# Gated mix of linear attention and a squared-ReLU block on one core: the second piece of the first chunks issued from ScalarE's queue

## The chip, the core and the metric

The kernel runs on one core of a Trainium2 chip. The metric is the device time in microseconds (us) of one execution; the kernel before was run three times. One further execution was taken by the hardware profiler, and all lines of a profile shown here come from such an execution. Engines are TensorE (PE in the profile, its weight loads PEld), VectorE (DVE), ScalarE (ACT), GpSimd (POOL) and SyncE (SP); SPq and ACTq are the instructions with which SyncE and ScalarE issue transfers.

## The reference

The input x has 2048 rows (tokens) of 448 numbers, all float32. Two branches are computed from it and mixed with a gate for each token:

```python
x = A_x
g = _sigmoid((x * gate_w).sum(-1, keepdims=True))
a = _A_ref(x, A_wqkv, A_wo)                    # linear attention, 16 heads of 28
b = _B_ref(x, B_w1, B_b1, B_w2, B_b2)          # relu(x @ w1 + b1)**2 @ w2 + b2, hidden width 1792
return g * a + (1 - g) * b
```

In the attention branch q and k go through phi(t) = where(t > 0, t + 1, exp(t)) + 1e-6; then kv = sum over tokens of phi(k) v, z = sum of phi(k), and the output is phi(q) kv / (phi(q) z + 1e-6), multiplied by wo.

## The kernel before

All inputs are float32. Each operand of a matmul is split into a high part, rounded to the matmul's type float32r, and a low part, the rest; a product is then three matmuls (high by high, low by high, high by low). ScalarE mostly makes the high part (`split_hi`, line 66, or line 68 on VectorE), VectorE the low part (`split_lo`, line 71).

The 448 input features lie in four chunks of up to 128 (c = 0 to 3, the last one holds 64 features twice), the tokens in four blocks of 512 (b = 0 to 3), and the hidden width in 14 tiles of 128. The program opens with the up projection (x by w1) of block 0: six hidden tiles (`NS = 6`), each with a PSUM bank of its own, `first[0]` to `first[5]`, called h_ps in the profile. Chunk 0 goes first, with 128-row matmuls at lines 685 and 216, then chunk 1; chunks 2 and 3 follow from a queue of parts that `work_off` emits at line 300, in two halves of 64 rows. After that come keys, down projection, attention and the other blocks; the stores end the program.

The order in which each engine runs its instructions is the order in which the code is written (`manual_schedule`). At the head of the program it is this:

- TensorE runs 14 matmuls on constants (line 177, `warm_ps`), which need no data.
- SyncE issues the loads through `load` (line 59). The first two (lines 181 to 183) are the pieces of xw. Piece n is a tile `xwr` of 128 partitions by 512 numbers: 256 columns of x, chunk 0 (the tokens of one half of block 0), beside 256 columns of w1, chunk 0 (two of the hidden tiles 0 to 3). Then follow w1 for the hidden tiles 4 to 6, chunk 0 (`w1r` from w1b), and for chunks 1 to 3 a piece of x (`xr`) and two of w1 (`w1r` from w1a and w1b).
- Lines 680 to 688 take piece 0 and then piece 1: VectorE casts the x columns to `xh` (line 681), ScalarE makes the high part of the two weight tiles (line 683), TensorE multiplies hidden tiles 0 and 1 by these columns (line 685), VectorE subtracts to get `xl` (line 686), and TensorE multiplies with that (line 688, by way of line 216). Line 690 then makes the low part of the weights from both pieces, line 691 splits the third load, and lines 692 to 696 run the rest of chunk 0 on six hidden tiles.

Each engine works in order. A transfer tells its end by one of eight semaphores in turn, so that SyncE's eighth and later transfers each wait until the one that had the semaphore before has landed.

Of the kernel before, what the change touches and what calls it, by code (L numbers as in the profile page):

```python
# [33 lines left out]
def gated_mix_kernel(ctx: ExitStack, tc: tile.TileContext, xw, xt, xn, wk, wq, wv, wo, w1a, w1b, w2, b1, b2, gw,  # L34
                     kvmask, out):
    nc = tc.nc
    act, dve, pool, pe, sp = nc.scalar, nc.vector, nc.gpsimd, nc.tensor, nc.sync
# [15 lines left out]
    def slot(shape, dt, name):  # L53
        return work.tile(shape, dt, name=name, tag="s", bufs=NSLOT)
# [3 lines left out]
    def load(dst, src):  # L58
        loader[0].dma_start(out=dst, in_=src)
# [70 lines left out]
    def load_w1(h, g, c):  # L130
        w1_raw[h, g, c] = slot([P, (TB, 3 * P)[g]], F, f"w1r{h}{g}{c}")
        load(w1_raw[h, g, c], (w1a, w1b)[g][h, c])
# [47 lines left out]
    xw_raw = []  # L180
    for n in range(2):
        xw_raw.append(slot([P, TB], F, f"xwr{n}"))
        load(xw_raw[n], xw[n])
    load_w1(0, 1, 0)
    for c in range(1, 4):
        load_x(0, c)
# [763 lines left out]
```

## Time and profile before

| | us |
|---|---|
| median of 3 runs | 420.62 (420.17 to 420.63) |
| profiled execution, its own time | 420.09 |
| its span, first to last instruction | 418.3 |
| TensorE busy in the span | 414.2 |
| VectorE, ScalarE, GpSimd busy | 274.6, 173.2, 87.5 |
| first use of xw piece 0, piece 1 (from the span's start) | 3.43, 4.42 |

The granted clock of TensorE is given as 1.000 over the span. In a row of the timeline stand the start, the duration, the engine, the line, the operation with the tile written and the tiles read, the count of instructions merged, and in brackets the idle time of the engine before it and what ended it. In the list of waits stand the engine and line that waited, for whom, and three numbers: us in total, times, the longest in us. A busy TensorE is not TensorE at its peak, since matmuls overlap; the distance from start to start tells the pace.

### The profile page before, as it was taken

What the parts mean: (1) busy time and instruction counts of PE and PEld (TensorE: products, weight loads), DVE (VectorE), ACT (ScalarE), POOL (GpSimd) and SP (SyncE); (2) the same over time, 40 slices, a digit from 0 to 9 for tenths busy, and PEclk for the clock granted to TensorE, in tenths of its full rate; (3) what the DMA queues carried; (4) which work ended last, traced back from release to release, by engine and by line L of the source; (5) the groups of instructions that cost most, each with busy time, mean ns of one, the idle gap of its engine ahead of it and who ended that gap; (6) DMA issues with size and microseconds to landing.
All of it is one profiled execution on the core that took longest, in us unless ns stands there. A gap on an engine that the chain in (4) does not pass through costs nothing.

```text
span 418.3 us, 9312 instructions
## 1 busy us (share of the span) xinstructions
PE 414.2 (99%) x3836; PEld 402.4 (96%) x3836; DVE 274.6 (66%) x520; ACT 173.2 (41%) x305; POOL 87.5 (21%) x166
## 2 busy tenths in 40 slices
PE   9999999999999999999999999999999999999996
PEld 6899999999999999999999999999999999999996
DVE  5887737682476827576379886678843975558734
ACT  6965335451044621445234653325530363314720
POOL 0015300140003400035830498200402013110000
PEclk9999999999999999999999999999999999999999
DMA  8805500050001610006541155210402013010002
GB/s 272 259 8 146 182 2 5 6 194 2 2 5 32 198 46 2 3 19 203 171 133 43 31 89 154 66 44 2 127 2 88 2 23 107 19 70 2 2 2 88
DMA packets 12634, 29.81 MB, mean 71 GB/s; under 512 B 3136, under 2 KB 6176, under 8 KB 12592
## 3 DMA queue, kind: packets, MB, share of 16 engines
q0 software_dynamic: 8416, 22.76, 18.2%
q1 hardware_dynamic: 4032, 6.37, 4.7%
q8 instruction: 30, 0.49, 0.5%
q14 instruction: 12, 0.10, 0.1%
q10 hardware_dynamic: 144, 0.10, 0.1%
HBM read 23.28 MB, written 4.20 MB: 66 GB/s over the span
## 4 chain that ended last, share of the span: by engine, by line
PE 99%; DVE 0%; issue 0%
PE o_ps L300 30%; PE h_ps L300 30%; PE k_ps L300 9%; PE g_ps L300 8%; PE a_ps L300 8%; PE q_ps L300 7%; PE h_ps L216 2%; PE o_ps L881 1%; PE kv_ps L300 1%; PE warm_ps L177 1%; PE m_ps L300 1%; PE last_ps L82 0%; PE h_ps L685 0%; DVE last L898 0%
## 5 line engine op out<-in xcount | busy, mean ns | idle before, releaser
L300 PE MATMUL h_ps<-xh,w 64*128 64x512 f32 x709 | 160.0, 387 | 0.0
L300 PE MATMUL o_ps<-w,hh 64*128 64x448 f32 x848 | 153.0, 359 | 0.0
L300 PEld LDWEIGHTS o_ps<-w,hh 64*128 64x128 f32 x848 | 124.9, 184 | 2.6
L300 PE MATMUL h_ps<-xl,w 64*128 64x512 f32 x395 | 124.8, 387 | 0.0
L300 PE MATMUL o_ps<-w,hl 64*128 64x448 f32 x424 | 124.3, 360 | 0.0
L300 PEld LDWEIGHTS h_ps<-xh,w 64*128 64x128 f32 x709 | 107.5, 184 | 0.9 <-ACT w L66 0.4
L300 PEld LDWEIGHTS o_ps<-w,hl 64*128 64x128 f32 x424 | 74.7, 184 | 1.4
L300 PEld LDWEIGHTS h_ps<-xl,w 64*128 64x128 f32 x395 | 65.0, 184 | 0.2
L221 ACT ACTIVATE hr<-h_ps,b_s 128x512 f32<-128x512 f32 x56 | 38.1, 680 | 61.0 <-PE h_ps L300 61.0
L300 PE MATMUL k_ps<-wk_s,xh 64*128 64x512 f32 x216 | 59.1, 386 | 0.0
L68 DVE CAST hh<-hr 128x512 fp32r<-128x512 f32 x56 | 23.5, 420 | 33.7 <-ACT hr L222 32.7
L300 PE MATMUL k_ps<-wk_s,xl 64*128 64x512 f32 x120 | 40.3, 386 | 0.0
L71 DVE TENSOR_TENSOR hl<-hr,hh 128x512 fp32r<-128x512 f32 x56 | 39.0, 697 | 1.9
L300 PE MATMUL q_ps<-xh,wq_s 64*128 64x512 f32 x160 | 39.7, 387 | 0.0
L425 POOL DMA_DIRECT2D qd<-q x16 | 8.8, 550 | 147.1 <-DVE q L421 147.1
L300 PE MATMUL a_ps<-m_s,qh 64*128 64x448 f32 x216 | 38.6, 359 | 0.0
L222 ACT ACTIVATE hr<-hr 128x512 f32<-128x512 f32 x56 | 35.4, 633 | 1.8
L300 PE MATMUL g_ps<-pl,nh 64*128 64x448 f32 x128 | 36.1, 359 | 0.0
L300 PE MATMUL g_ps<-ph,nh 64*128 64x448 f32 x128 | 36.1, 358 | 0.0
L300 PEld LDWEIGHTS k_ps<-wk_s,xh 64*128 64x128 f32 x216 | 35.2, 184 | 0.4
L300 PEld LDWEIGHTS a_ps<-m_s,qh 64*128 64x128 f32 x216 | 33.0, 184 | 1.4
L300 PE MATMUL a_ps<-m_s,ql 64*128 64x448 f32 x120 | 32.3, 359 | 0.0
(132 smaller groups left out, 685.0 us busy)
## 6 DMA issues: line engine op xcount, KB each, us to landing
xr<-in_xt POOLq DMA_DIRECT2D x24, 256.0 KB, 3.0
xnr<-in_xn POOLq DMA_DIRECT2D x16, 224.0 KB, 3.8
out<-out POOLq DMA_DIRECT2D x12, 224.0 KB, 2.2
w2r<-in_w POOLq DMA_DIRECT2D x9, 224.0 KB, 3.0
m_s<-m POOLq DMA_DIRECT2D x24, 56.0 KB, 2.5
w2r<-in_w SPq DMA_DIRECT2D x5, 224.0 KB, 6.8
wkr<-in_wk SPq DMA_DIRECT2D x4, 256.0 KB, 4.3
w1r<-in_w1a POOLq DMA_DIRECT2D x4, 256.0 KB, 3.5
```

The lines of the kernel that those rows point to most:

```text
L68: eng.tensor_copy(hi, src)
L71: eng.tensor_tensor(lo, src, f32(hi), op=ALU.subtract)
L177: pe.matmul(warm_ps[:, :256], warm[:, :P], warm, start=True, stop=True)
L216: ins = pe.matmul(ps, a, m, start=(c == 0 and n == 0), stop=False)
L221: act.activation(r, ps, AF.Relu, bias=b1_s[:, f:f + 1])
L222: act.activation(r, r, AF.Square)
L300: ins = pe.matmul(out, a, m, start=start, stop=stop)
L425: pool.dma_start(out=q_t[b][i], in_=q)
L881: ins = pe.matmul(total.ps[:, :D], a[:, i * P:(i + 1) * P], w[:, k], start=False, stop=f == NF - (3 if i == 3 else 1) and n == 2)
```

## The change

The second piece of xw is issued by ScalarE, as the first instruction of its program, and no longer by SyncE. The first piece stays on SyncE, now by a direct call in place of `load`. Sizes, tiles and all that is computed are the same.

```diff
     xw_raw = []
     for n in range(2):
         xw_raw.append(slot([P, TB], F, f"xwr{n}"))
-        load(xw_raw[n], xw[n])
+        (sp, act)[n].dma_start(out=xw_raw[n], in_=xw[n])
     load_w1(0, 1, 0)
```

SyncE's program at its head, as a difference (xwr_102 is piece 0, xwr_104 piece 1, w1r_106 the up weights of the hidden tiles 4 to 6 for chunk 0, xr_1_108 chunk 1 of x):

```order
 L946 UNCONDITIONAL_BRANCH
-L59 DMA xwr_102<-in_xw 128x512
-L59 DMA xwr_104<-in_xw 128x512
+L183 DMA xwr_102<-in_xw 128x512
 L59 DMA w1r_106<-in_w1b 128x384
 L59 DMA xr_1_108<-in_xt 128x512
```

One issue leaves, and every load behind it stands one place earlier.

ScalarE's program at its head before, with the semaphores that an instruction waits for (DMAHW0 is piece 0's landing, DMAHW1 piece 1's; w_00 is the split weight tile of the hidden tiles 0 to 3, w_01 that of 4 to 6):

```order
L946 UNCONDITIONAL_BRANCH [waits barrier_Pool_Activation_PE_DVE_SP_release]
L66 ACT_TABLE_LOAD
L66 ACTIVATE w_00_166<-xwr_102 128x128 [waits DMAHW0_49]
L66 ACTIVATE w_00_166<-xwr_102 128x128
L66 ACTIVATE w_00_166<-xwr_104 128x128 [waits DMAHW1_49]
L66 ACTIVATE w_00_166<-xwr_104 128x128
L66 ACTIVATE w_01_185<-w1r_106 128x384 [waits DMAHW2_49]
```

and with the change:

```order
L946 UNCONDITIONAL_BRANCH [waits barrier_Pool_Activation_PE_DVE_SP_release]
L183 DMA xwr_104<-in_xw 128x512
L66 ACT_TABLE_LOAD
L66 ACTIVATE w_00_166<-xwr_102 128x128 [waits DMAHW0_49]
L66 ACTIVATE w_00_166<-xwr_102 128x128
L66 ACTIVATE w_00_166<-xwr_104 128x128 [waits DMAHW1_49]
L66 ACTIVATE w_00_166<-xwr_104 128x128
L66 ACTIVATE w_01_185<-w1r_106 128x384 [waits DMAHW2_49]
```

The issue of piece 1 stands ahead of the table load; ScalarE's other instructions keep their order, and so do all of TensorE's, VectorE's and GpSimd's.

## Prediction

> **What bounds the kernel now.** I read the page first: its totals and its chain of waits.
>
> ```profile
> span 418.3 us, 9312 instructions
> PE 414.2 (99%) x3836; PEld 402.4 (96%) x3836; DVE 274.6 (66%) x520; ACT 173.2 (41%) x305; POOL 87.5 (21%) x166
> PE 99%; DVE 0%; issue 0%
> ```
>
> TensorE is busy from its first to its last instruction, and the chain that ended last runs through it alone. So this change can move the end only by moving TensorE's stream. The list of waits, taken for TensorE's weight loads over the whole program, says how often anything holds that stream up:
>
> ```profile
> PEld L177 <- issue: 0.8, 1, 0.8
> PEld h_ps L685 <- ACT w L66: 0.4, 1, 0.4
> PEld h_ps L300 <- ACT w L66: 0.4, 1, 0.4
> PEld o_ps L881 <- issue: 0.3, 1, 0.3
> PEld h_ps L685 <- DVE xh L68: 0.2, 1, 0.2
> PEld h_ps L216 <- DVE xl L71: 0.2, 1, 0.2
> ```
>
> There are six waits in 418 us. Three of them (L685 twice, L216 once) belong to the first chunk, which is what the two pieces of xw feed. Next I read the timeline of the first 14 us (start, duration, engine, line, operation):
>
> ```profile
> 0.75 1.28 ACT L66 ACT_TABLE_LOAD   x1 [0.75 <-PEq L942]
> 0.75 0.86 SPq L59 DMA_DIRECT2D xwr<-in_xw  x2
> 0.78 3.00 PE L177 MATMUL warm_ps<-const-bfloat16-1.0 128*128 128x256 bf16 x14 [0.78 <-PEq L942]
> 1.65 0.42 SPq L59 DMA_DIRECT2D w1r<-in_w1b  x1
> ...
> 3.43 0.51 ACT L66 ACTIVATE w<-xwr 128x128 fp32r<-128x128 f32 x2 [1.40 <-DMA xwr<-in_xw]
> 3.43 0.29 DVE L68 CAST xh<-xwr 128x256 fp32r<-128x256 f32 x1 [3.43 <-DMA xwr<-in_xw]
> 3.76 0.42 DVE L71 TENSOR_TENSOR xl<-xwr,xh 128x256 fp32r<-128x256 f32 x1
> 3.84 0.34 PEld L685 LDWEIGHTS h_ps<-xh,w 128*128 128x128 f32 x2 [0.40 <-ACT w L66]
> ...
> 4.42 0.51 ACT L66 ACTIVATE w<-xwr 128x128 fp32r<-128x128 f32 x2 [0.48 <-DMA xwr<-in_xw]
> 4.42 0.29 DVE L68 CAST xh<-xwr 128x256 fp32r<-128x256 f32 x1 [0.24 <-DMA xwr<-in_xw]
> ...
> 4.75 0.42 DVE L71 TENSOR_TENSOR xl<-xwr,xh 128x256 fp32r<-128x256 f32 x1
> 5.09 0.75 DVE L71 TENSOR_TENSOR w<-xwr,w 128x256 fp32r<-128x256 f32 x2
> 5.23 0.51 PE L216 MATMUL h_ps<-xl,w 128*128 128x256 f32 x2
> 5.37 0.53 ACT L66 ACTIVATE w<-w1r 128x384 fp32r<-128x384 f32 x1 [0.44 <-DMA w1r<-in_w1b]
> 5.57 0.63 PE L216 MATMUL h_ps<-xh,w 128*128 128x512 f32 x2
> 5.93 0.56 DVE L71 TENSOR_TENSOR w<-w1r,w 128x384 fp32r<-128x384 f32 x1
> 6.50 1.30 PE L216 MATMUL h_ps<-xh,w 128*128 128x512 f32 x5
> 6.52 0.63 ACT L66 ACTIVATE xh<-xr 128x512 fp32r<-128x512 f32 x1 [0.62 <-DMA xr<-in_xt]
> 7.18 0.69 DVE L71 TENSOR_TENSOR xl<-xr,xh 128x512 fp32r<-128x512 f32 x1 [0.69 <-ACT xh L66]
> 12.63 0.39 PE L216 MATMUL h_ps<-xh,w 128*128 128x512 f32 x1
> 12.94 0.50 PE L300 MATMUL h_ps<-xh,w 64*128 64x512 f32 x2
> ```
>
> The reader should see the relay. Piece 0 lands and is used at 3.43, piece 1 at 4.42. After each landing VectorE casts x and subtracts: piece 1's low part ends at 4.75 + 0.42 = 5.17, and TensorE takes it at 5.23. From 5.57 matmuls start one behind the other, 0.23 us apart: the five at 6.50 span 1.30, the last lasts 0.39 like the single one at 12.63, so (1.30 - 0.39) / 4. At the step from 12.63 to 12.94 only 0.31 - 0.23 = 0.08 us is spare, and the list of waits has nothing behind it but 0.3 us near the end. So **whatever the first chunk loses or wins at 5.23 arrives at the end almost whole**; there is no idle time later in TensorE's stream that could swallow more than about 0.1 us.
>
> **Are the transfers limited by issuing or by moving bytes?** The summary of the tile xwr and the table of windows answer it (in the table: the window, each engine's busy time, the granted clock, the DMA engines' busy share, GB/s):
>
> ```profile
> L59 SPq DMA_DIRECT2D xwr<-in_xw x2: 381/401/421, 0.7 to 1.2; - x2
> DMA to landing us min/median/max: 2.7/2.9/3.2
> 2.00:3.00 1.00, 1.00 (x7) 0.72 (x5) 0.00 (x0) 0.03 (x1) 0.00 (x0) 1.00 0.97 270
> 3.00:4.00 1.00, 0.92 (x6) 0.47 (x5) 0.53 (x2) 0.51 (x2) 0.00 (x0) 1.00 0.99 324
> 4.00:5.00 1.00, 0.97 (x6) 0.70 (x6) 0.73 (x3) 0.51 (x2) 0.00 (x0) 1.00 1.06 293
> 8.00:9.00 1.00, 1.00 (x7) 0.81 (x5) 0.97 (x2) 0.89 (x2) 0.00 (x0) 1.00 1.05 393
> ```
>
> The second issue starts about 0.45 us behind the first, yet its data lands 0.99 us behind (4.42 - 3.43). Between 2 and 5 us the DMA engines are 97 to 106% busy. So piece 1 waits behind piece 0's bytes, not for SyncE: 0.5 MB take what they take. In-order service is worth something here, because the early piece is whole at 3.43 while the other still moves.
>
> **The change part by part.** *SyncE:* one issue less at its head, so the nine loads behind it issue about 0.45 us earlier. That is worth nothing by itself: the queue already runs ahead of busy DMA engines, and the chunk 1 data they bring has cover (VectorE's first use is 7.18 + 0.69 = 7.87, while TensorE comes to it at about 8.55: 6.50 plus nine matmuls of 0.23).
>
> *ScalarE:* one issue more, ahead of its table load. The nearest row is ScalarE's own issue at the end of the program, beside SyncE's:
>
> ```profile
> L899 SPq DMA_DIRECT2D out<-last x1: 357/357/357, 415.0 to 415.0; - x1
> L899 ACTq DMA_DIRECT2D out<-last x1: 372/372/372, 415.5 to 415.5; - x1
> ```
>
> So 0.37 to 0.42 us. The table load moves from 0.75 to about 1.2 and ends at about 2.5, under the 1.40 us that ScalarE sits idle before 3.43. Cost nothing; without that cover it would be 0.4 us.
>
> *The landings:* this carries the sum. Both pieces are now issued at 0.75, from two queues, to DMA engines that are full. If the engines take turns between the queues, each piece gets half the rate and both are complete about when the second is now. Piece 1 wins nearly nothing; **piece 0 loses up to 0.99 us**. Everything on ScalarE and VectorE waits in order for piece 0 first. VectorE's work from piece 0's landing to piece 1's low part is then unbroken: 0.75 (3.43 to 4.18), 0.04 between instructions, 0.75 (4.42 to 5.17), together 1.54 us. With T0 for piece 0's landing the low part ends at T0 + 1.54, and TensorE shifts by T0 + 1.54 - 5.17 = **T0 - 3.63**, as long as piece 1 lands within 0.79 us of piece 0.
>
> T0 from both sides: at the present rate both land at 4.42, a shift of +0.79. If two queues move bytes at the 393 GB/s of the 8 to 9 us row instead of the 296 that the rows from 2 to 5 us average, 524 kB take 1.33 us instead of 1.77, so T0 = 3.98 and the shift is +0.35. ScalarE's piece may also start later by d: then, roughly, T0 = 4.42 - d and T1 = 4.42 + d, and the shift is the larger of 0.79 - d and d, which is never under 0.40. I take the middle, T0 = 4.20: **+0.57 us**.
>
> What hides the rest: ScalarE's four weight casts end at 4.20 + 1.04 = 5.24, before its next data at 5.37. VectorE runs 0.57 late into 5.93, and its idle 0.69 before 7.18 takes that up; without it, chunk 1 would be late by as much, still ahead of TensorE's need. TensorE's own delay has no cover. The sum for the profiled execution is 420.09 (span 418.3 and 1.8 around it) + 0.57 = 420.66; that execution lies 0.53 under the median of the runs, 420.62, so the forecast is 420.62 + 0.57 = **421.2 us, 0.14% longer**. A measurement of this kernel tells 0.2% (0.84 us) from no change, so that counts as no change.
>
> **The rivals.**
>
> *A, both pieces come early.* If the queues do not hinder each other, both land at 3.43: the low part ends at 3.43 + 1.54 = 4.97, a gain of 0.20 us, 420.4. VectorE's chain forbids more. For it: the rate of 270 to 324 GB/s early against 393 later leaves room. Against it: the busy share of 97% and more. 10%.
>
> *B, piece by piece as now.* The engines finish the first queue's rows before they turn to the other: 3.43 and 4.42 stay, shift 0, 420.6. For it: piece 0 has only 128 rows of 2 KB, few for each DMA engine. Against: nothing in the trace shows two loading queues at once. 15%. In the Trainium skill, "DMA: Bandwidth & Descriptors", section "Queues, rings and completion order", the engine changes queue only at the end of a packet, typically 9 to 17 descriptors; by that rule a piece could pass undivided and this rival would hold. No row here shows it.
>
> *C, ScalarE's piece is overtaken.* If its queue starts late enough that the up-weight load of SyncE (w1r) also goes ahead, piece 1 takes that load's landing, 5.37 in place of 4.42: shift 0.95, 421.6, slower. It decides from 0.84 us of lateness, T1 at 5.26. For it: SyncE's loads now follow 0.45 us sooner. Against: the ACTq row is as quick as the SPq row. 13%.
>
> *D, TensorE's pace drops.* The summary of line 177 gives the warm-up's matmuls (shortest, median and longest time in ns, first and last start):
>
> ```profile
> L177 PE MATMUL warm_ps<-const-bfloat16-1.0 x14: 278/417/417, 0.8 to 3.5; 128*128 128x256 bf16 x14
> ```
>
> Fourteen starts of 256 columns between 0.78 and 3.5 are 0.21 us apart, while 512 columns later take 0.23: TensorE begins at half pace. Its idle time after the warm-up grows from under 0.1 us (3.78 to the load at 3.84) to about 0.8 (3.78 to 3.84 + 0.77). If that gap keeps or puts it back at half pace for another stretch of 2.7 us, the price is 1.35 us on top of 0.57: 422.5, slower by 0.45%. For it: the warm-up ends right where the data now arrives. Against: TensorE already tolerates its idle first 0.78 us and gaps of 0.2 to 0.4. 10%. In the Trainium skill, "TensorE: Matmul & The Clock Gate", section "Part 1: The HAM clock gate", the full clock comes after a busy window of about 3.4 us and goes after an idle one; a gap of 0.8 us is no idle window, so by that rule the rival holds only where the first full window falls across the gap. The half pace until 3.5 agrees with it.
>
> **How the numbers follow.** Forecast (shared engines, +0.35 to +0.79) 52%, A 10%, B 15%, C 13%, D 10%. The likeliest gives 421.2. The range must hold A with some scatter (the runs shown differ by 0.46 us) and C, and may leave D out: 420.3 to 422.0. Slower by over 0.2%: D 10%, most of C 11%, and the part of the forecast that scatter lifts over 0.84, 8%: 29%. Faster by over 0.2%: no mechanism reaches it, 3% for what I do not see. The rest, 68%, lies within.
>
> **What would show it.** In the changed profile's timeline: ScalarE's and VectorE's first use of xwr between 3.98 and 4.42 instead of 3.43 is the sharing step; 3.43 with 4.42 unchanged is B; 3.43 for both is A. VectorE's second cast following its first subtraction without a wait for DMA shows the 1.54 us chain; a DMA wait there up to 5.3 is C. TensorE's first 512-column matmul at 5.57 + 0.57 = about 6.1, and the step to L300 at about 13.5 instead of 12.94, show that the delay is kept. Matmuls of 512 columns further apart than 0.23 us after 6 us would be D. The forecast is wrong if piece 0 still lands at 3.43, or if the later stream starts late by another amount than the first chunk.

## The result and the profile after

Over ten runs each, the changed kernel has a median of 421.95 us (420.54 to 422.51), the kernel before 420.25 (419.94 to 420.63). The ratio is 1.0032 with a 95% interval of 1.0024 to 1.0041: slower, by more than the 0.2% that this kernel's measurement can tell from no change. The ten times of the changed kernel do not lie around their median. Three are at 420.54, 420.55 and 420.80, seven between 421.77 and 422.51, and none between.

The profiled execution of the changed kernel took 422.41 us, with a span of 420.6: one of the seven. Its list of waits for TensorE's weight loads (us in total, times, longest):

```profile
PEld h_ps L685 <- ACT w L66: 1.1, 1, 1.1
PEld L177 <- issue: 0.8, 1, 0.8
PEld h_ps L300 <- ACT wk_s L66: 0.4, 1, 0.4
PEld o_ps L881 <- issue: 0.3, 1, 0.3
```

The three small waits of the first chunk have become one of 1.1 us. From the timeline of the changed kernel's first 16 us, a selection of its rows (start, duration, engine, line, operation):

```profile
0.75 0.38 SPq L183 DMA_DIRECT2D xwr<-in_xw  x1
0.75 0.41 ACTq L183 DMA_DIRECT2D xwr<-in_xw  x1
0.78 3.15 PE L177 MATMUL warm_ps<-const-bfloat16-1.0 128*128 128x256 bf16 x14 [0.78 <-PEq L942]
1.19 1.28 ACT L66 ACT_TABLE_LOAD   x1 [1.19 <-PEq L942]
4.18 0.91 ACT L66 ACTIVATE w<-xwr 128x128 fp32r<-128x128 f32 x4 [1.71 <-DMA xwr<-in_xw]
4.18 0.29 DVE L68 CAST xh<-xwr 128x256 fp32r<-128x256 f32 x1 [4.18 <-DMA xwr<-in_xw]
4.62 0.77 PE L685 MATMUL h_ps<-xh,w 128*128 128x256 f32 x2 [0.69 <-ACT w L66]
4.86 0.28 DVE L68 CAST xh<-xwr 128x256 fp32r<-128x256 f32 x1
5.17 0.43 DVE L71 TENSOR_TENSOR xl<-xwr,xh 128x256 fp32r<-128x256 f32 x1
6.47 1.05 PE L216 MATMUL h_ps<-xh,w 128*128 128x512 f32 x2
7.32 1.05 PE L216 MATMUL h_ps<-xl,w 128*128 128x512 f32 x2
8.17 1.90 PE L216 MATMUL h_ps<-xh,w 128*128 128x512 f32 x5
10.15 0.62 PE L216 MATMUL h_ps<-xh,w 128*128 128x512 f32 x2
15.24 0.50 PE L300 MATMUL h_ps<-xh,w 64*128 64x512 f32 x2
```

Piece 0 is used at 4.18 instead of 3.43, and VectorE's second cast at 4.86 shows no wait: piece 1 was there by then. TensorE has nothing to do from 3.93 to 4.62. After that comes what the profile before did not have: pairs of 512-column matmuls start 0.85 us apart (6.47, 7.32, 8.17), 0.43 for each, nearly twice the 0.23 of before. Only from about 9.4 us (8.17 and three steps of 0.43) do they come 0.23 apart. The step to line 300 stands at 15.24 instead of 12.94, 2.30 us late, and the span is longer by the same 2.3: nothing later gave or took any. The views give the granted clock as 1.000 in this profile too, so in them the half pace is seen in the starts of the matmuls alone.

The DMA engines of the changed kernel, by stage (window, busy time of each engine, granted clock, busy share, GB/s), and then its two queues between 2.5 and 4 us (packets, MB, share of 16 engines; q1 is SyncE's queue, q10 ScalarE's):

```profile
2.00:3.00 1.00, 1.00 (x7) 0.73 (x5) 0.00 (x0) 0.47 (x1) 0.00 (x0) 1.00 0.62 176
3.00:4.00 1.00, 0.93 (x5) 0.32 (x3) 0.00 (x0) 0.00 (x0) 0.00 (x0) 1.00 1.04 397
```

```profile
q1 hardware_dynamic: 155, 0.27, 48.2%
q10 hardware_dynamic: 142, 0.26, 45.4%
```

Between 2.5 and 4 us the two queues get the DMA engines about half and half. The first microsecond of moving is slower than before (176 GB/s against 270), the second faster (397 against 324).

### The profile page after: what moved, and what is told of

It is laid out like the page before. It is cut to its first block, busy times and chain, and to the rows that moved or that the text cites. A ratio compares the mean times of both kernels' runs of the same rounds, so it can differ in the third digit from the quotient of the medians.

```text
span 420.6 us, 9312 instructions
## 1 busy us (share of the span) xinstructions
PE 415.9 (99%) x3836; PEld 404.0 (96%) x3836; DVE 274.6 (65%) x520; ACT 173.0 (41%) x305; POOL 87.0 (21%) x166
## 4 chain that ended last, share of the span: by engine, by line
PE 98%; DMA 1%; DVE 0%; ACT 0%; issue 0%
PE o_ps L300 30%; PE h_ps L300 30%; PE k_ps L300 9%; PE g_ps L300 8%; PE a_ps L300 8%; PE q_ps L300 7%; PE h_ps L216 2%; PE o_ps L881 1%; DMA xwr<-in_xw 1%; PE kv_ps L300 1%; PE m_ps L300 1%; PE last_ps L82 0%; PE h_ps L685 0%; DVE last L898 0%; ACT w L66 0%
```

## The experiments

There were two questions. Why do seven of ten executions lose 1.5 to 2.3 us when the late data alone should cost 0.55 (4.18 - 3.63)? And is piece 0 late because bytes of piece 1 move beside it?

### Filling the idle time with warm-up matmuls

```diff
-    for _ in range(14):
+    for _ in range(18):
         pe.matmul(warm_ps[:, :256], warm[:, :P], warm, start=True, stop=True)
```

> The changed kernel with 18 instead of 14 warm-up matmuls, so that TensorE has work from 0.78 to about 4.57 us and is idle only briefly before the first chunk's matmuls at about 4.62. Theory P (pace): the profile of the changed kernel starts 512-column matmuls 0.43 us apart until 9.43 us and 0.23 after, because the idle time from 3.72 to 4.62 made TensorE keep its half pace for a further stretch; the late data alone costs 0.55 us (first use of both pieces at 4.18, T0 - 3.63). With the gap filled, P expects no execution with the half pace beyond about 7 us, all runs between 420.4 and 421.3, median about 420.8. Rival L (landing): the whole 1.7 us comes from the data's lateness and what follows from it on ScalarE and VectorE; it expects no change from the changed kernel, median about 422.0 with runs up to 422.5.

Measured: median 420.62, eleven runs between 420.43 and 421.19, ratio to the kernel before 1.0011 (1.0003 to 1.0020). In its profile:

```profile
0.78 4.00 PE L177 MATMUL warm_ps<-const-bfloat16-1.0 128*128 128x256 bf16 x18 [0.78 <-PEq L942]
4.08 0.91 ACT L66 ACTIVATE w<-xwr 128x128 fp32r<-128x128 f32 x4 [1.62 <-DMA xwr<-in_xw]
5.90 0.62 PE L216 MATMUL h_ps<-xh,w 128*128 128x512 f32 x2
6.81 1.30 PE L216 MATMUL h_ps<-xh,w 128*128 128x512 f32 x5
13.25 0.50 PE L300 MATMUL h_ps<-xh,w 64*128 64x512 f32 x2
```

The data is as late as in the changed kernel (4.08), but five matmuls span 1.30 us again, and line 300 comes at 13.25. Four matmuls whose result nobody uses took the slow group away. Theory P holds here and rival L falls.

The edit was then run again on another chip, together with the changed kernel unaltered.

> The changed kernel unaltered, on the same chip as its form with 18 warm-up matmuls, since the share of executions near 422 differed between runs with the same idle gap (7 of 10, 4 of 12, 1 of 11). Theory P: two groups of times, one at 420.3 to 421.2 (full pace in time) and one at 421.5 to 422.6 (half pace for a further stretch); how many fall into each is not forecast, at least one of each in ten. Rival L (data's lateness alone): one group with no gap in it.

> The changed kernel with 18 warm-up matmuls, on the same chip. Theory P: one group only, 420.3 to 421.2, no execution at 421.5 or above, and TensorE's 512-column matmuls 0.23 us apart by 7 us in the profile. Rival L: the same spread as the changed kernel unaltered.

Measured: the changed kernel 420.40 once and 421.50 to 422.51 five times (median 422.09, ratio 1.0038, 1.0023 to 1.0053); with 18 warm-ups eleven runs from 420.49 to 421.23 (median 420.55, ratio 1.0012, 1.0003 to 1.0021). In this second profile with 18 warm-ups, of an execution of 420.98 us, the half pace still lasted to 6.3 us: the added matmuls take the slow group away, but not all of the half pace in every execution. This time the profile of the unaltered kernel fell on the one quick execution:

```profile
4.08 0.91 ACT L66 ACTIVATE w<-xwr 128x128 fp32r<-128x128 f32 x4 [1.61 <-DMA xwr<-in_xw]
4.52 0.50 PE L685 MATMUL h_ps<-xh,w 128*128 128x256 f32 x2 [0.73 <-ACT w L66]
6.81 1.30 PE L216 MATMUL h_ps<-xh,w 128*128 128x512 f32 x5
13.25 0.50 PE L300 MATMUL h_ps<-xh,w 64*128 64x512 f32 x2
```

It is the same program with data that is late as well (4.08 against 4.18) and about the same idle time (0.73 against 0.69), but at full pace: line 300 at 13.25 and not 15.24. The two profiles of one kernel differ by 1.99 us there, and by 422.41 - 420.40 = 2.01 us in time. As 0.10 of that goes with the later landing, the price of the half pace is about 1.9 us.

### The same idle time without the change

```diff
-    for _ in range(14):
+    for _ in range(10):
         pe.matmul(warm_ps[:, :256], warm[:, :P], warm, start=True, stop=True)
```

in the kernel before, all loads on SyncE.

> The kernel before, both pieces on SyncE's queue, with 10 instead of 14 warm-up matmuls: TensorE is idle from about 2.9 to 3.87 us, a gap like that of the changed kernel, while no transfer and no other engine's instruction moves. Theory P (an idle gap of about 1 us in the warm-up keeps TensorE at half pace for longer): pieces used at 3.43 and 4.42 as before, half pace until some point between 6.4 and 9.8 us, which costs half of the time from 5.3 to that point, 0.55 to 2.2 us; median about 421.4, runs between 420.5 and 422.5. Rival L (only when the data comes matters): 420.2 to 420.6 as before.

Measured: median 421.48, six runs from 420.90 to 422.14; ratio 1.0027 (1.0015 to 1.0038). Its profile, of an execution that took 421.05:

```profile
0.78 2.29 PE L177 MATMUL warm_ps<-const-bfloat16-1.0 128*128 128x256 bf16 x10 [0.78 <-PEq L942]
3.36 1.16 ACT L66 ACTIVATE w<-xwr 128x128 fp32r<-128x128 f32 x4 [1.33 <-DMA xwr<-in_xw]
3.80 0.77 PE L685 MATMUL h_ps<-xh,w 128*128 128x256 f32 x2 [0.72 <-ACT w L66]
6.49 1.06 PE L216 MATMUL h_ps<-xl,w 128*128 128x512 f32 x2
```

Piece 0 comes at 3.36, on time; the idle time is 0.72 us, as in the changed kernel; and the 512-column matmuls start 0.43 apart (the pair that spans 1.06). Idle time of this length ahead of the first chunk is enough to lose a microsecond, with no transfer touched.

### Issuing piece 1 later

The first try put a tiny activation ahead of ScalarE's issue (the lines that define `side` and `one` are left out):

```diff
...
+        if n:
+            act.activation(side[:, :1], one, AF.Copy)
         (sp, act)[n].dma_start(out=xw_raw[n], in_=xw[n])
```

> The changed kernel, but ScalarE issues piece 1 only after its table load and one tiny activation, at about 2.1 us instead of 0.75. Theory S (the two queues share the DMA engines row by row, so piece 0 is late because piece 1 moves beside it): piece 0 moves alone for most of its way and is used at 3.4 to 3.7 instead of 4.18; piece 1 then shares with the loads behind piece 0 and is used at 4.7 to 5.4, later than the 4.42 of before, and VectorE's second cast waits for it. TensorE's first 512-column matmul at about 5.9 to 6.5. The time is 420.25 plus 0.3 to 1.0 where TensorE is at full pace by then, and more in executions that keep half pace. Rival Q (a piece issued by ScalarE, or the first one on SyncE beside it, is slow for a reason of its own, such as the start of the queue): piece 0 is used at about 4.18 again, or piece 1 stays 3.4 us behind its issue, which is 5.5.

Its profile shows that the edit did not do what it was meant to:

```profile
0.74 1.28 ACT L185 ACT_TABLE_LOAD   x1 [0.74 <-PEq L945]
0.81 0.38 ACTq L186 DMA_DIRECT2D xwr<-in_xw  x1
2.03 0.20 ACT L185 ACTIVATE side<-const-float32-1.0 128x1 f32<-128x1 f32 x1
4.13 0.98 ACT L66 ACTIVATE w<-xwr 128x128 fp32r<-128x128 f32 x4 [1.89 <-DMA xwr<-in_xw]
```

The issue, third in the order of the code, went out at 0.81, during the table load and ahead of the activation. So this was the changed kernel once more: piece 0 at 4.13, eight runs from 420.18 to 420.88, four from 422.05 to 422.42 (median 420.71, ratio 1.0021, 1.0008 to 1.0034). Two further edits held the issue back by a real wait, on an instruction that first writes to the tile of piece 1, in one case VectorE's, in the other ScalarE's:

```diff
+        if n:
+            dve.memset(xw_raw[n], 0.0)
         (sp, act)[n].dma_start(out=xw_raw[n], in_=xw[n])
```

> The changed kernel, with ScalarE's issue of piece 1 held back: VectorE first clears the tile (one memset of 128x512), and the issue waits for that, about 0.5 us later than SyncE's issue of piece 0. Theory S (both queues share busy DMA engines): for the first half microsecond piece 0 moves alone, so it is used between its two known places, 3.43 alone and about 4.15 fully shared: 3.6 to 4.0; piece 1 at 4.2 to 4.6. VectorE's last low part at about 5.2 to 5.5, TensorE's first 512-column matmul at 5.5 to 5.9 in executions at full pace. Time 420.1 plus 0.1 to 0.5, and up to 2 us more where half pace is kept. Rival Q (piece 0 is late because a second queue is used at all, not because bytes move beside it): piece 0 at about 4.15 again.

```diff
...
+        if n:
+            act.activation(xw_raw[n][:, :1], one, AF.Copy)
         (sp, act)[n].dma_start(out=xw_raw[n], in_=xw[n])
```

> The late issue once more, now with a wait that holds it: a one-column activation writes the tile of piece 1 ahead of the issue, so that ScalarE issues piece 1 only at about 2.2 to 2.4 us, behind its table load. By then SyncE has issued piece 0 and two or three loads behind it. Theory S: piece 0 moves alone or beside SyncE's own later loads that queue behind it, and is used at 3.3 to 3.6; piece 1 shares from its first byte with SyncE's backlog and is used at 5.2 to 6.0, so VectorE's second cast waits for it and TensorE idles from about 4.5 to 5.6: this is the rival of the prediction in which ScalarE's piece is overtaken. Time 420.1 plus 0.8 to 1.6, and more where half pace is kept. Rival Q: piece 0 at about 4.1 though nothing of piece 1 moves yet.

The profile with VectorE's wait, then the one with ScalarE's:

```profile
1.44 0.38 ACTq L185 DMA_DIRECT2D xwr<-in_xw  x1
3.46 0.51 ACT L66 ACTIVATE w<-xwr 128x128 fp32r<-128x128 f32 x2 [0.33 <-DMA xwr<-in_xw]
4.55 0.51 ACT L66 ACTIVATE w<-xwr 128x128 fp32r<-128x128 f32 x2 [0.59 <-DMA xwr<-in_xw]
```

```profile
2.27 0.38 ACTq L186 DMA_DIRECT2D xwr<-in_xw  x1
3.52 0.51 ACT L66 ACTIVATE w<-xwr 128x128 fp32r<-128x128 f32 x2 [1.29 <-DMA xwr<-in_xw]
7.27 0.51 ACT L66 ACTIVATE w<-xwr 128x128 fp32r<-128x128 f32 x2 [3.24 <-DMA xwr<-in_xw]
```

With piece 1 issued 0.69 us after piece 0, piece 0 is back at 3.46 and piece 1 at 4.55. Eight of ten runs lie between 420.18 and 421.13, but two at 423.67 and 424.19, and no profile shows why (median 420.54, ratio 1.0024, 1.0000 to 1.0048). Issued at 2.27, piece 1 lands only at 7.27, 5.0 us later; all four runs are at 425.08 to 425.50 (ratio 1.0120, 1.0105 to 1.0135). That is the prediction's overtaken piece, and far dearer than either theory said. Of the 5.1 us some 2.9 are the late piece itself (7.27 - 4.42); in the profile TensorE, idle again while it waited, also kept the half pace until 13.5 us. The lateness is not only a matter of turns, since the DMA engines themselves slow down there:

```profile
4.00:5.00 1.00, 1.00 (x4) 0.86 (x4) 0.28 (x1) 0.04 (x1) 0.00 (x0) 1.00 0.82 127
```

Why they moved 127 GB/s at that point stays open. What both runs settle is that piece 0 is on time as soon as piece 1 does not start beside it; using a second queue does not make it late by itself.

### Another load beside piece 0, halves, other addresses, exchanged queues

Here the pieces stay on SyncE, and ScalarE issues the third load:

```diff
+    loader[0] = act
     load_w1(0, 1, 0)
+    loader[0] = sp
```

> Both pieces of xw stay on SyncE's queue as before; ScalarE's queue instead issues the third load (up weights of chunk 0 for hidden tiles 4 to 6, 192 KB) at the head of its program. Nothing that TensorE needs first has moved. Theory S: any 192 KB that move beside piece 0 delay it: piece 0 used at 3.8 to 4.1 instead of 3.43, piece 1 at 4.3 to 4.7, the third load used before it is needed. Time 420.1 plus 0.2 to 0.6, more where half pace is kept. Rival Q (only the piece issued by ScalarE suffers): piece 0 at 3.4 and piece 1 at about 4.4 as before, time as before.

Measured: piece 0 at 3.58, 0.15 late, nearer to Rival Q's 3.4 than to the 3.8 to 4.1 that Theory S asked for; ratio 1.0002 (0.9993 to 1.0011), ten runs from 420.12 to 420.70, no slow group. The profile's stage row is the difference:

```profile
2.00:3.00 1.00, 1.00 (x7) 0.74 (x5) 0.00 (x0) 0.47 (x1) 0.00 (x0) 1.00 0.89 308
```

308 GB/s between 2 and 3 us against 176. So sharing is not the whole of piece 0's lateness: with the two pieces of xw side by side the transfers also start slower. Whether the addresses do that was tried by moving piece 1 in memory:

```diff
-        (sp, act)[n].dma_start(out=xw_raw[n], in_=xw[n])
+        (sp, act)[n].dma_start(out=xw_raw[n], in_=xw[n, :P])
...
+    a["xw"] = np.pad(a["xw"], ((0, 0), (0, 10), (0, 0)))
```

> The changed kernel, with ten unused rows of 2 KB behind each piece in memory, so that piece 1 begins 276 KB instead of 256 KB behind piece 0; the transfers, tiles and queues are the same. In the changed kernel and its two variants with both pieces at 0.75 us the DMA engines moved only 125 to 193 GB/s between 2 and 3 us, in all other kernels 250 to 308. Theory M (two queues that read rows exactly 256 KB apart hinder each other in memory): 250 to 300 GB/s between 2 and 3 us, both pieces used by 3.6 to 3.9, time 420.1 to 420.6 and rarely above 421.5. Theory S alone (equal sharing of busy engines, and a slow start whatever the addresses): 125 to 200 GB/s between 2 and 3 us, piece 0 used at 4.05 to 4.2 as in the changed kernel, times spread from 420.2 to 422.5.

Measured: 227 GB/s between 2 and 3 us and piece 0 at 4.09. The landing is Theory S's, and the rate, though above what Theory S said, stays under Theory M's 250: 20 KB more between the addresses did not cure it, and the slow start stays unexplained. The median was 420.51 (ratio 1.0001, 0.9992 to 1.0011), with one of eleven runs, the profiled one, at 422.16 and at half pace until about 8.5. So on this chip the slow group was rare although the profile shows nearly the same idle time (0.61).

```diff
-        (sp, act)[n].dma_start(out=xw_raw[n], in_=xw[n])
+        (act, sp)[n].dma_start(out=xw_raw[n], in_=xw[n])
```

> The changed kernel with the queues exchanged: ScalarE issues piece 0, SyncE piece 1. Theory S (equal sharing): piece 0 used at 4.0 to 4.2 again, about the same as in the changed kernel, 420.4 to 422.5 us. Rival Q (a transfer on ScalarE's queue has a late start of its own, while SyncE's keeps its pace): piece 0 used at 4.3 or later, piece 1 already there.

One execution, 420.82 us: piece 0, now from ScalarE, is used at 4.50, and both landings took 3.6 to 3.7 us from their issue. These are the signs of Rival Q: by the semaphores in the trace piece 1, from SyncE, had landed at 4.31 and piece 0 at 4.48. Both pieces still arrive close together, as with equal sharing, but 0.3 later than Theory S said. The packets in the trace show the late start: SyncE's queue moves its first at 1.76, ScalarE's at 2.80, though both were issued at 0.75. In the changed kernel these are 2.16 and 2.65, with landings at 4.16 and 4.33. There the piece that comes last is the one needed last, so the lateness costs nothing.

```diff
-        (sp, act)[n].dma_start(out=xw_raw[n], in_=xw[n])
+        for q, rows in zip((sp, act), HALVES):
+            q.dma_start(out=xw_raw[n][rows], in_=xw[n][rows])
```

> Each piece is cut into two halves of 64 partitions; SyncE issues the upper halves, ScalarE the lower halves, piece 0 ahead of piece 1 on both queues. All bytes are the same. Theory S: piece 0 is no longer beside piece 1, and both queues bring it together, so it is used at 3.3 to 3.6 and piece 1 at 4.0 to 4.4, if the 397 GB/s of the changed kernel's 3 to 4 us window holds rather than the 324 of before. TensorE's first 512-column matmul at 5.2 to 5.6, as before or up to 0.3 us earlier; time 419.9 to 420.4. Rival Q (a transfer from ScalarE's queue comes late by itself): both pieces are used at 4.0 or later, time 420.8 to 422.

The attempt at a faster kernel failed: median 422.72 (421.39 to 424.80), ratio 1.0059 (1.0039 to 1.0079). Its profile:

```profile
0.74 1.46 SPq L184 DMA_DIRECT2D xwr<-in_xw  x2
3.69 1.28 ACT L66 ACT_TABLE_LOAD   x1 [3.69 <-DMA xwr<-in_xw]
5.62 0.29 DVE L68 CAST xh<-xwr 128x256 fp32r<-128x256 f32 x1 [1.15 <-DMA xwr<-in_xw]
```

Two issues take 1.46 us instead of 0.86, piece 1 comes at 5.62, and the table load, which had lain under the wait for the data, now stands behind that wait at 3.69. Several things went wrong at once, the half pace until 10.2 us among them, so it tells nothing about sharing. None of the edits beat the kernel before.

## Why the prediction was right and where it was wrong

The measured 421.95 us lies inside the range of 420.3 to 422.0, and this is luck. The range left out D, the drop of TensorE's pace, and it is D that raised the median by more than a microsecond; five of the ten executions lie above 422.0. None of the ten lies within 0.3 us of the forecast's 421.2.

**What bounds the kernel.** TensorE's stream does, and it has no slack behind the first chunk: shown. 2.30 us at line 300 became 2.3 us of span in the execution at 422.41, 0.31 us (13.25 - 12.94) became 0.3 in the one at 420.40.

**The landings.** T0 was taken as 4.20 and measured 4.18 and 4.08 in the two profiles of the changed kernel, inside the bounds of 3.98 and 4.42. The split between the queues is even (48.2% and 45.4%), and piece 1 gains hardly anything, as forecast (it landed at 4.33; before it was used at 4.42). The working was right in result and incomplete in cause: a lower rate in the first microsecond and a higher one in the second nearly cancel, and another load beside piece 0 cost it only 0.15 us. Rival B, piece by piece, falls with T0 and with the queues' packets in the same 1.5 us. By the packet rule of the Trainium skill, "DMA: Bandwidth & Descriptors", section "Queues, rings and completion order", a piece could have passed undivided; the measured T0 decides against that here.

**VectorE's chain.** It was put at 1.54 us from landing to piece 1's low part and took 1.42 (4.18 to 5.60), because a cast starts a little before the subtraction ahead of it ends. ScalarE's issue took 0.41 us, and the table load, from 1.19 to 2.47, stayed under the wait for data as forecast.

**The cost at full pace.** +0.57 was forecast. The quick execution that was profiled is 0.3 longer in span than the profile of before, and this follows from the prediction's own chain: with T0 at 4.08, T0 - 3.63 is 0.45, and the chain that is 0.12 shorter leaves 0.33. With 18 warm-ups the cost is 0.11 to 0.12% (1.0003 to 1.0021), some 0.5 us, in which some half pace is left. So the term was right in kind, and in size a little too large.

**The step that failed** is the one that left TensorE's pace out of the sum: rival D was given 10%, with the words that TensorE already tolerates its idle first 0.78 us and gaps of 0.2 to 0.4. It tolerates 0.7 us more in some executions only: of the 16 timed ones of the unaltered changed kernel 12 are at 421.5 or above, so there D was the likeliest case and not a side case, and the chances of 68% for no change and 29% for slower were the wrong way round. In the two variants with the same late pieces the share was smaller (4 of 12 and 1 of 11). D's price was 1.35 us on top of the late data, at a total of 422.5; it measured about 1.9 between two profiles of one kernel, and the slow group's times are 421.5 to 422.5. The price was low because the half pace lasted from 4.62 to 9.4, not for 2.7 us; the total came out near since the chunk's own delay was smaller.

The Trainium skill, "TensorE: Matmul & The Clock Gate", section "Part 1: The HAM clock gate", says that full clock needs a window of about 3.4 us of sustained work, and that these windows run freely, so that it depends on the execution where one begins. The traces show such windows here, and that the work in them need not be unbroken. Beside the rows, each stored trace holds a list of stretches with the clock granted in them. The first stretch, at full clock, begins at 3.51 us in the profile of before, at 3.53 in the quick one of the changed kernel and at 9.43 in the one of 422.41 us, each time where the matmuls change pace. Ahead of it nothing is listed, and the views count that as 1.000; so neither the 1.000 given for the kernel before nor that for the changed one means full clock from the start. In all 13 profiles this stretch lasts a whole multiple of 3.413 us (122 of them before, 121 in the changed kernel at 422.41), so windows of that length can be counted back from its beginning. Time without matmuls is counted here with each matmul lasting as long as the step to the next (0.21 us for 256 columns at half pace):

| profile | window before full clock | idle in it, us | window ahead of that | idle in it, us |
|---|---|---|---|---|
| before | 0.09 to 3.51 | 0.69 | ended ahead of the first matmul | all |
| changed, 420.40 us | 0.11 to 3.53 | 0.67 | ended ahead of the first matmul | all |
| changed, 422.41 us | 6.02 to 9.43 | 0.00 | 2.61 to 6.02 | 1.04 |
| before with 10 warm-ups | 4.15 to 7.57 | 0.00 | 0.74 to 4.15 | 1.11 |
| changed with 18 warm-ups | 1.27 to 4.68 | 0.00 | mostly ahead of the first matmul | 2.93 |

In the execution at 420.40 a window ended before the idle time; in the one at 422.41 a window held all of it, and the full clock came only with the next. The other profiles fit: a window with at most 0.69 us idle was followed by full clock in all 13, one with 0.84 or more never. So what sorts the profiled executions is where the windows fall, shown in the traces. The prediction had named this condition ("only where the first full window falls across the gap") but put no number on it. As an estimate from these figures, a window has to end between about 3.5 and 4.4 us for a quick execution, 0.9 of 3.41 us or about one placement in four; 4 of 16 agree with that, the variants' 8 of 12 and 10 of 11 do not, and why the windows fell better there stays open.

## What to carry to other kernels

Where two transfers are needed one after the other and the DMA engines are already full, as here, putting them on two queues makes the first one late and the second hardly earlier: look at the landings and the busy share, not at the issue times. Where TensorE is warmed up by dummy matmuls, these should reach to the moment the real data comes; whoever delays the data must lengthen the warm-up, or pay for the gap a second time in pace. When the times of a kernel fall into two groups, take a profile of each: here one median hid 0.3 to 0.6 us in one group and 1.5 to 2.3 us in the other.

## What was not expected of the hardware

After an idle time of 0.7 us TensorE stayed at half pace for up to 4.8 us more, while the views gave the granted clock as 1.000; whether this happens depends on where windows of 3.413 us fall. An issue on ScalarE's queue overtook the activation in front of it (0.81 against 2.03 us). ScalarE's queue moved its first packet 0.3 to 1.1 us behind SyncE's in the eight profiles in which both queues were given a load of 128 rows at 0.74 to 0.81 us; with the halves it was SyncE's that began later, by 0.3. And a 256 KB transfer that was issued 1.5 us behind the other queue's first one needed 5.0 us to land, in a stretch in which the DMA engines moved 127 GB/s.
